# Summing the two parts of VectorE's exponentials with accumulating DMAs in a two-layer transformer kernel

## The chip, the cores and the metric

The kernel runs on one core of a Trainium2 chip. Five engines work beside each other, each with an instruction queue of its own that it follows in order: TensorE (PE: matmuls, and PEld: the loading of their weights), ScalarE (ACT), VectorE (DVE), GpSimd (POOL) and SyncE (SP, which only issues DMAs). Sixteen DMA engines move the data. Engines wait for each other by semaphores. The metric is the device time of one execution in microseconds (us).

## What is computed

Two transformer layers, one after the other, with the same weights, over 2048 rows of 448 numbers in bf16. Each layer is an attention block and a dense block, each behind a layer norm:

```python
qkv = (x @ wqkv).reshape(B, S, 3, H, Dh)          # B=1, S=2048, H=16, Dh=28
scores = jnp.einsum("bhqd,bhkd->bhqk", q, k) * scale
p = _softmax(scores, axis=-1)
o = jnp.einsum("bhqk,bhkd->bhqd", p, v)           # then @ wo
...
h = jnp.einsum("bsd,df->bsf", x, w1) + b1         # F=1792
r = jnp.where(h > zero, h, zero)
out = jnp.einsum("bsf,fd->bsd", r * r, w2) + b2
...
x = x + _A_ref(_layernorm(x), A_wqkv, A_wo)
x = x + _B_ref(_layernorm(x), B_w1, B_b1, B_w2, B_b2)
```

and the last two lines once more. The exponentials of the softmax are the largest single piece: 2 layers x 16 heads x 2048 x 2048 of them.

## The kernel before

**Tiling.** The 16 heads are four groups of four; each head has 32 rows of the 128 partitions. The queries are cut in blocks of 256 rows (the last ones of layer two in 128). A *pass* is one query block of one head group over some of the keys. A *unit* or *part* is one head's 512 columns of scores: 128 keys on the partitions, two key blocks of 256 queries beside each other. There are 2048 parts.

**A group.** `s_stream` puts two or three parts into a group. TensorE writes their scores into one PSUM tile `sc` of three banks (line 1154; two such tiles exist), and ScalarE turns the tile into exponentials `pt` in SBUF with one instruction (line 1192: 1024 columns for two parts, 1536 for three). TensorE may compute the same scores twice (`again`, limited by MORE), which keeps it at work. The value matmuls (line 1380) multiply the exponentials with the values and sum over the keys in PSUM, four heads beside each other.

**VectorE's parts.** In some groups the third part does not go to ScalarE. `apart` decides it: by lists of group numbers (FORCE, SKIP), by VectorE's load and by the memory cells that are free. For such a part VectorE builds the exponential from the bits of the number. Line 1216 (or 1214) reads the scores and writes a 16-bit integer `z`. From there the exponential is made as a **sum of two bf16 tiles**: `x2`, a product, and `z`, in which only the exponent bits are left. There are two ways to them. In `a_rest` GpSimd (at times VectorE) computes a bent copy (line 1263), a fraction (line 1269) and the new `z` (line 1274), and VectorE multiplies (line 1278). In `a_whole` VectorE does all of it: lines 1232, 1236 and 1239. Which one it is depends on PLIM, a limit on the work queued for GpSimd. Each of `z` and `x2` lies in a cell of 512 columns: in buffers of their own (`v_c`), in parts of K, Q and V tiles that are not needed at the time, or, for `z`, in the unused third of `pt`.

**The two reads.** Nothing adds the two tiles. TensorE multiplies both with the same values and lets PSUM add: `z` with the other parts at line 1380, and `x2` in batches of its own at line 1345, when at least XMIN heads have one ready. The variables `known`, `more` and `batch` in `p_stream` keep the account of the second read.

**The order of the work.** A planner in the kernel's file simulates all engines with a price for each operation and writes out one fixed order for each engine. Every operation is an `Op` with an engine, a duration, what it depends on, and the cells it holds (`acq`, `rel`). `lat` is a time between its end and the moment when others may use it. Streams of operations have priorities; of those that can go on, the one that could start first is taken. A set of constants steers the choice (how full VectorE may be, how long parts wait, how many cells are kept), and `PACE` changes them from group to group. An operation with `port=True` takes turns between VectorE and GpSimd. On the chip only the order and the semaphores are left, not the planned times.

**DMAs.** SyncE issues the loads, the stores of the output, and for each pair of head groups three small steps for the softmax's denominator (lines 1480, 1491, 1499). GpSimd issues none. Besides its part of the exponentials GpSimd computes the root of the layer norms (line 673).

**Stages.** An opening until the first exponential; then attention of both layers with the dense blocks mixed in; and a tail in which the last rows go through the dense block. The last 80 parts (STOP) all go to ScalarE.

Of the kernel before, what the change touches and what calls it, by code (L numbers as in the profile page):

```python
# [13 lines left out]
ALU = mybir.AluOpType  # L14
# [16 lines left out]
PLIM = 99.0  # L31
OVER = 0.0825
EDUR = 0.617
# [5 lines left out]
XMIN = 4  # L39
HELD = 0.14  # L40
# [105 lines left out]
FORCE = (22, 27, 31, 36, 64, 104, 108, 120, 122, 156, 162, 192, 196, 233, 235, 237, 254, 263, 287, 292, 301, 306,  # L146
         329, 341, 392, 408, 430, 445, 466, 501, 515, 553, 556, 567, 577, 593, 598, 602)
SKIP = (20, 29, 46, 135, 184, 195, 216, 222, 242, 262, 280, 282, 320, 321, 378, 388, 395, 404, 406, 409, 416, 418,
        433, 440, 446, 479, 500, 512, 526, 544, 574, 601, 609, 621, 622, 646, 652, 663)
PACE = {  # L150
    0: {'BUSY': 0.95, 'LOW': 0.7, 'CHUNK': 1, 'EV': 2.9, 'FAR': 6, 'KEEP': 5, 'LAG': 8, 'LEAD': 18, 'MARGIN': 3,
         'MORE': 3, 'PRE': 0.5, 'SLACK': 0.7, 'SPAN': 8, 'TB': 2.4, 'TB2': 2.4, 'V_AGE': 5, 'V_LAST': 3, 'V_PAST':
         2, 'C_PRIO': 1.6, 'V_PRIO': 4, 'V_LATE': 2.6, 'V_WAIT': 5, 'ASIDE': 1, 'XMIN': 4, 'HOLD': 6, 'LADD': 0.05,
         'RES': 2, 'RES2': 2, 'TASIDE': -0.2, 'EPRIO': 2.6, 'SPARE': 0, 'NEAR': 3, 'SOON': 1, 'VGAP': 0.03, 'PWAIT':
         0.3, 'PNEAR': 0.2, 'PORTP': 1, 'PLIM': 99.0},
    8: {'LEAD': 12, 'BUSY': 0.9, 'PLIM': 2},
    16: {'SPAN': 11},
    24: {'LAG': 3},
    32: {'PLIM': 2.6, 'EV': 3.5},
    40: {'TB2': 3.0},  # L160
    42: {'BUSY': 0.95, 'CHUNK': 3, 'EV': 2.9, 'LAG': 8, 'LEAD': 18, 'MORE': 1, 'SPAN': 8, 'TB': 1.6, 'TB2': 2.4,
         'V_PRIO': 8.5},
    56: {'BUSY': 1.0, 'LAG': 3},
    64: {'NEAR': 9, 'ASIDE': 0.2, 'LADD': 0.1},
    72: {'V_AGE': 4},
    88: {'V_AGE': 3},
    112: {'C_PRIO': 1.2, 'HOLD': 5},
    120: {'LEAD': 10, 'LAG': 12, 'SPARE': 3, 'ASIDE': 2},
    128: {'TB': 2.0, 'MORE': 3},
    136: {'PRE': 1.2, 'MARGIN': 6},  # L170
    144: {'EPRIO': 4},
    152: {'CHUNK': 1, 'VGAP': 0},
    160: {'BUSY': 0.95, 'V_PRIO': 4, 'V_PAST': 3},
    168: {'RES': 1, 'C_PRIO': 2.1, 'LOW': 1.0},
    176: {'EV': 2.2, 'TB2': 2.0, 'LOW': 0.5},
    192: {'PORTP': 0.3, 'SOON': 0.6},
    200: {'CHUNK': 2, 'PRE': 0.3},
    208: {'PNEAR': 0.25, 'V_AGE': 6},
    216: {'NEAR': 3},
    248: {'EPRIO': 6},  # L180
    256: {'ASIDE': 0},
    264: {'MARGIN': 10},
    280: {'PORTP': 2},
    288: {'HOLD': 6},
    296: {'TB': 1.0, 'PNEAR': 0.15},
    304: {'SPAN': 6},
    312: {'BUSY': 1.0},
    320: {'LEAD': 12, 'MARGIN': 6},
    328: {'V_LATE': 6},
    336: {'LOW': 1.0},  # L190
    360: {'PNEAR': 0.05, 'TB': 2.4, 'V_LATE': 2.6, 'V_AGE': 3},
    368: {'C_PRIO': 1.6},
    376: {'PNEAR': 0.15, 'V_PRIO': 8.5},
    384: {'XMIN': 3, 'LEAD': 18},
    392: {'CHUNK': 3},
    400: {'KEEP': 6, 'ASIDE': 4, 'V_AGE': 6, 'BUSY': 0.9},
    408: {'PWAIT': 0.6, 'MORE': 1},
    424: {'RES': 2, 'BUSY': 1.0},
    440: {'HEAT': 0.6, 'WINDOW': 3.4, 'CHUNK': 2},
    456: {'V_AGE': 5, 'TB': 1.3},  # L200
    480: {'TB': 1.6, 'PORTP': 0.3, 'PLIM': 2},
    488: {'LADD': 0.2, 'HOLD': 4},
    496: {'MARGIN': 3, 'PNEAR': 0.35},
    504: {'PWAIT': 0.3},
    512: {'KEEP': 4, 'EV': 2.9},
    520: {'V_AGE': 4, 'C_PRIO': 1.2, 'HOLD': 5},
    528: {'PRE': 0.8},
    536: {'XMIN': 4, 'SPAN': 15, 'ASIDE': 2, 'PRE': 0.3},
    544: {'V_AGE': 5, 'EV': 2.2},
    552: {'PORTP': 1, 'LEAD': 12, 'FAR': 17, 'PRE': 0},  # L210
    560: {'V_LATE': 6, 'VGAP': 0.03},
    568: {'SPARE': 0, 'NEAR': 9},
    576: {'SOON': 1.5, 'PNEAR': 0.15},
    584: {'PLIM': 1.3, 'LAG': 3, 'V_WAIT': 3},
    592: {'KEEP': 6, 'V_LAST': 2.2},
    600: {'V_AGE': 8},
    608: {'EV': 1.3, 'LOW': 0.8},
    616: {'PRE': 1.2, 'BUSY': 0.95, 'V_PAST': 2, 'FAR': 6},
    624: {'LADD': 0.1, 'BUSY': 0.9},
    648: {'PRE': 0.5, 'SPAN': 20, 'EV': 3.5, 'ASIDE': 0.2},  # L220
    656: {'ASIDE': 1, 'SLACK': 0.4},
    672: {'SOON': 1, 'ASIDE': 0.2},
    680: {'SLACK': 0.7},
# [183 lines left out]
def kernel(  # L407
# [819 lines left out]
    def a_whole(gi, c, unit):  # L1227
# [14 lines left out]
        o = Op("DVE", 0.42, close, deps=[h], sets=("x", gi), port=True)  # L1242
        w = Op("DVE", TDUR, whole, deps=[o], sets=("w", gi), port=True)
# [6 lines left out]
        left[0] -= 0.34  # L1250

    def a_rest(gi, c, unit):
# [39 lines left out]

    norm_done = {}
    rows_done = set()
# [400 lines left out]
```

## Time and profile before

| | before |
|---|---|
| time, median of 2 runs | 803.53 us (803.46 to 803.6) |
| time of the profiled execution | 803.48 us |
| its span, first to last instruction | 801.7 us |
| TensorE's granted clock | 1.00 |
| instructions | 29246 |
| DMA traffic | 18.13 MB, 23 GB/s over the span |
| exponentials on ScalarE (line 1192) | 683, 776.6 us |
| parts on VectorE (lines 1214, 1216) | 337 |

A share of the span tells how full an engine is, not whether it sets the end. For that the idle time of each engine has to be placed: where it lies, and what ended it. Groups of instructions come with their busy time, the mean length of one in ns and the engine's idle time just before them. Neighbouring instructions of one engine may overlap in the records; a busy time of a group counts covered time once, a mean does not. Instructions that only issue a DMA or wait for a semaphore are not counted as busy. "issue" is time in which an engine waited for nothing that the profile shows.

### The profile page before, as it was taken

The page shows a single profiled execution, that of the slowest core. Times are in us where ns is not written, and L with a number is a line of the kernel's source. Part 1 is how long each engine was busy: PE and PEld are TensorE (multiplying, and loading weights), DVE is VectorE, ACT ScalarE, POOL GpSimd, SP SyncE. Part 2 cuts the span into 40 slices and gives each one's busy share as a digit, 9 for nine tenths or more (in the row PEclk, how much of TensorE's full clock was granted, in tenths as well). Part 3 has the DMA queues.
Part 4 walks back from the last instruction along what each step waited for, and adds up shares of the span by engine and source line. Part 5 has one row for each costly group of instructions (what it writes and reads, how often), then busy time and mean ns, then how long its engine had stood idle before and what let it go on. Part 6 is the DMA issues. An engine that isn't in the chain of part 4 may idle for free.

```text
span 801.7 us, 29246 instructions
## 1 busy us (share of the span) xinstructions
PE 778.7 (97%) x12242; PEld 417.6 (52%) x12242; DVE 744.8 (93%) x1818; ACT 789.4 (98%) x702; POOL 454.7 (57%) x717
## 2 busy tenths in 40 slices
PE   9999989999999999999999999989999999999998
PEld 6555545544555545555455545445454544545666
DVE  8999999999999999999999998999999999989564
ACT  8999999999999999999999999999999999999995
POOL 3346777657676664544566657657665566654200
PEclk9999999999999999999999999999999999999999
DMA  9300010000000000000000000011100000000100
GB/s 250 86 2 2 5 34 23 17 16 16 17 3 16 16 16 16 3 16 15 2 3 2 3 2 2 15 32 30 33 11 22 21 28 21 22 23 9 27 8 19
DMA packets 32480, 18.13 MB, mean 23 GB/s; under 512 B 17818, under 2 KB 31899, under 8 KB 32348
## 3 DMA queue, kind: packets, MB, share of 16 engines
q1 hardware_dynamic: 32204, 16.16, 7.4%
q8 instruction: 95, 1.56, 0.8%
q14 instruction: 37, 0.30, 0.1%
q10 hardware_dynamic: 144, 0.11, 0.0%
HBM read 13.98 MB, written 2.06 MB: 20 GB/s over the span
## 4 chain that ended last, share of the span: by engine, by line
PE 41%; ACT 33%; DVE 17%; issue 8%; DMA 0%; POOL 0%; ACTq 0%; DVEq 0%
ACT pt L1192 33%; PE mt L809 19%; PE sc L1154 12%; PE oT L1380 7%; DVE pt L1216 2%; DVE r L1584 2%; PE oT L1345 1%; DVE pt L1214 1%; DVE V_sb L1591 1%; DVE K_sb L1278 1%; DVE v_c L1278 1%; DVE v_c L1216 1%; PE tp L712 1%; DVE x_sb L1513 1%; PE sc L809 1%
## 5 line engine op out<-in xcount | busy, mean ns | idle before, releaser
L1192 ACT ACTIVATE pt<-sc 128x1536 bf16<-128x1536 f32 (+1 forms) x683 | 776.6, 1292 | 1.2 <-PE sc L1154 0.9
L1154 PE MATMUL sc<-Q_sb,K_sb 32*128 32x256 bf16 (+1 forms) x4652 | 279.6, 265 | 15.7 <-ACT pt L1192 13.5
L1154 PEld LDWEIGHTS <-K_sb 32*128 32x128 bf16 x4652 | 101.1, 92 | 186.3 <-issue 118.3
L1380 PE MATMUL oT<-pt,V_sb 128*32 128x256 bf16 (+1 forms) x4000 | 167.8, 268 | 0.5 <-DVE Q_sb L828 0.3
L1380 PEld LDWEIGHTS <-V_sb 128*32 128x32 bf16 x4352 | 101.5, 96 | 45.3 <-issue 35.9
L809 PE MATMUL mt<-xnT,w 128*128 128x256 bf16 (+1 forms) x904 | 119.6, 270 | 0.9 <-DVE xnT L724 0.2
L1274 POOL TENSOR_SCALAR pt<-pt 128x512 int16<-128x512 int8 x131 | 83.9, 642 | 39.9 <-ACT pt L1192 5.7
L809 PEld LDWEIGHTS <-w 128*128 128x128 bf16 x952 | 78.0, 98 | 35.2 <-issue 26.4
L1216 DVE TENSOR_SCALAR pt<-sc 128x512 int16<-128x512 f32 x132 | 89.8, 684 | 2.3 <-PE sc L1154 1.6
L1584 DVE TENSOR_SCALAR r<-mt 128x512 bf16<-128x512 f32 (+1 forms) x107 | 73.0, 682 | 3.8 <-PE mt L809 3.4
L673 POOL TENSOR_TENSOR rstd<-mv,mhalf 128x2 f32<-128x2 f32 (+1 forms) x34 | 25.4, 747 | 76.4 <-DVE mv L676 48.2
L809 PE MATMUL mt<-w,V_sb 128*128 128x448 bf16 (+2 forms) x288 | 66.5, 345 | 0.0
L1274 POOL TENSOR_SCALAR v_c<-v_c 128x512 int16<-128x512 int8 x64 | 42.8, 668 | 24.5 <-DVE V_sb L1269 4.3
L1269 POOL TENSOR_SCALAR v_c<-pt 128x512 f16<-128x512 uint8 x57 | 37.8, 663 | 31.9 <-DVE K_sb L1263 5.8
L1513 DVE TENSOR_TENSOR x_sb<-x_sb,mt 128x448 bf16<-128x448 bf16 x61 | 37.4, 612 | 12.9 <-PE mt L809 12.6
L1216 DVE TENSOR_SCALAR v_c<-sc 128x512 int16<-128x512 f32 x69 | 46.6, 682 | 0.7 <-PE sc L1154 0.6
L648 DVE BATCH_NORM_STATS2 st<-x_sb 128x6 f32<-128x448 bf16 x63 | 38.9, 619 | 0.7 <-DMA x_sb<-in_A_x_dram 0.5
L809 PEld LDWEIGHTS <-V_sb 128*128 128x128 bf16 x302 | 25.4, 98 | 24.4 <-issue 10.0
L1345 PE MATMUL oT<-v_c,V_sb 128*32 128x256 bf16 (+1 forms) x298 | 35.0, 273 | 0.0
L1591 DVE TENSOR_TENSOR V_sb<-r 128x512 bf16<-128x512 bf16 x70 | 29.2, 421 | 3.0 <-ACT r L1582 2.8
L1274 POOL TENSOR_SCALAR K_sb<-K_sb 128x512 int16<-128x512 int8 x39 | 25.3, 650 | 11.2 <-DVE v_c L1278 2.4
L1269 POOL TENSOR_SCALAR K_sb<-pt 128x512 f16<-128x512 uint8 x35 | 23.9, 682 | 13.2 <-DVE pt L1216 4.3
(219 smaller groups left out, 1254.0 us busy)
## 6 DMA issues: line engine op xcount, KB each, us to landing
rec<-scr SPq DMA_DIRECT2D x54, 128.0 KB
out_dram<-x_sb SPq DMA_DIRECT2D x15, 112.0 KB
x_sb<-in_A_x_dram SPq DMA_DIRECT2D x7, 224.0 KB
w<-in_B_w_dram SPq DMA_DIRECT2D x1, 1568.0 KB
w<-in_B_w_dram SPq DMA_DIRECT2D x1, 1344.0 KB
dn<-oT_sb SPq DMA_DIRECT2D x54, 4.0 KB
V_sb<-in_A_wqkv_dram SPq DMA_DIRECT2D x4, 168.0 KB
scr<-dn SPq DMA_DIRECT2D x27, 8.0 KB
```

Source lines behind the costliest of these rows:

```text
L648: nc.vector.bn_stats(out=box["st"][:, :], in_=x_sb[:, t0 + j, :] if src is None else src())
L809: nc.tensor.matmul(box["t"][:, c0:c0 + n], lhsT=lhsT() if callable(lhsT) else lhsT, rhs=rhs, start=a, stop=b)
L1154: nc.tensor.matmul(dst[k][:, i * nt * P:(i + 1) * nt * P], lhsT=K_sb[l][rows, g, (kb + i) * P:(kb + i + 1) * P], rhs=Q_sb[rows, g, t0 * P: ...
L1192: t = nc.scalar.activation(out=pt[:, 0:n], in_=gbuf[gi]["sc"][:, 0:n], func=AF.Exp, scale=float(np.log(2.0)) * 2.0 ** -FRAC)
L1216: t = nc.vector.tensor_scalar(out=z.bitcast(DT.int16), in0=src, scalar1=2.0, scalar2=EXP_BIAS, op0=ALU.mult, op1=ALU.add)
L1269: on(e).tensor_scalar(out=box["f"], in0=gbuf[gi]["z"].bitcast(DT.uint8).rearrange("p (n t) -> p n t", t=2)[:, :, 0], scalar1=2.0 ** -9, sc ...
L1274: on(e).tensor_scalar(out=gbuf[gi]["z"].bitcast(DT.int16), in0=gbuf[gi]["z"].bitcast(DT.int8).rearrange("p (n t) -> p n t", t=2)[:, :, 1], ...
L1345: nc.tensor.matmul(box["t"][DHP * hh:DHP * hh + DHP, 0:n], lhsT=V_sb[l][:, kb + i, 4 * g + hh, :], rhs=gbuf[gi]["x2"][:, i * n:(i + 1) * n ...
L1380: nc.tensor.matmul(box["t"][DHP * hh:DHP * hh + DHP, 0:n], lhsT=V_sb[l][:, tb, 4 * g + hh, :], rhs=p, start=begin and j < G, stop=close an ...
L1513: nc.vector.tensor_tensor(out=x_sb[:, tb, lo:hi], in0=x_sb[:, tb, lo:hi] if src is None else src[:, lo:hi], in1=t[:, 0:hi - lo], op=ALU.add)
L1584: nc.vector.tensor_scalar(out=r[:, 0:w], in0=t[:, 0:w], scalar1=0.0, scalar2=None, op0=ALU.max)
L1591: nc.vector.tensor_tensor(out=h[:, 0:w // n, :], in0=r, in1=r, op=ALU.mult)
```

## The change

The two tiles of a VectorE part are added in memory, and the value matmuls read the sum once. A new function `summed` waits for the last of VectorE's operations of the part (`o` and `w`) and lets GpSimd issue a DMA that reads `x2` and adds it to `z` in SBUF. The planner prices this with ADUR = 0.62 us on GpSimd, `port=True`, and a token `("w", gi)` that comes ALAT = 2.0 us later; the value matmul at line 1380 waits for that token. The cell of `x2` becomes free with it. The token `("x", gi)` no longer exists, and with `not ACC` in `p_stream` no second read is ever put down, so the batches of line 1345 are gone.

The constants that steer the planner are chosen anew: FORCE goes from 38 to 22 groups, SKIP from 37 to 21, and PACE has fewer and other entries. PLIM is 1.2 from group 24 on, -1 from 408 to 527 (every part goes through `a_whole` there), and 1.2 again after that; before it was 2 or 2.6 from group 8 on and 1.3 from group 584 on.

```diff
+ACC = 1
+ADUR = 0.62
+ALAT = 2.0
...
-        o = Op("DVE", 0.42, close, deps=[h], sets=("x", gi), port=True)
-        w = Op("DVE", TDUR, whole, deps=[o], sets=("w", gi), port=True)
+        o = Op("DVE", 0.42, close, deps=[h], sets=() if ACC else ("x", gi), port=True)
+        w = Op("DVE", TDUR, whole, deps=[o], sets=() if ACC else ("w", gi), port=True)
...
+        if ACC:
+            pl.spawn(EPRIO, summed(gi, h, o, w))
+
+    def summed(gi, t, o, w):
+
+        def acc(e):
+            nc.gpsimd.dma_start(out=gbuf[gi]["z"], in_=gbuf[gi]["x2"], accum_op=ALU.add)
+        a = Op("POOL", ADUR, acc, deps=[o, w], port=True)
+        yield a
+        d = Op("-", 0.0, None, deps=[a], rel=t, lat=ALAT, sets=("w", gi))
+        d.dur = 0.0
+        yield d
...
-        w = Op(("POOL", "DVE"), (EDUR, 0.42), whole, deps=[t, h], sets=("w", gi), port=True)
-        o = Op("DVE", 0.42, close, deps=[t, h], rel=h, sets=("x", gi), port=True)
+        w = Op(("POOL", "DVE"), (EDUR, 0.42), whole, deps=[t, h], sets=() if ACC else ("w", gi), port=True)
+        o = Op("DVE", 0.42, close, deps=[t, h], rel=h, sets=() if ACC else ("x", gi), port=True)
...
+        if ACC:
+            pl.spawn(EPRIO, summed(gi, t, o, w))
...
-                        if k == 3 and gi not in known:
+                        if k == 3 and gi not in known and not ACC:
```

What the two built programs hold, by count:

| | before | after |
|---|---|---|
| exponentials on ScalarE, 1536 columns | 345 | 370 |
| exponentials on ScalarE, 1024 columns | 338 | 313 |
| parts on VectorE | 337 | 312 |
| of these wholly on VectorE (`a_whole`) | 67 | 194 |
| GpSimd's 128x512 operations (bent, fraction, whole) | 141, 249, 264 | 69, 118, 118 |
| accumulating DMAs issued by GpSimd | 0 | 312 |
| value matmuls | 5034 | 4352 |
| score matmuls (4096 without repeats) | 4652 | 4994 |

More of the change, by code (lines that the diff above doesn't have):

```diff
@@ L145 @@
 QP = 6
[L146 to L149, printed above, removed]
+FORCE = (56, 61, 87, 129, 131, 154, 238, 360, 397, 412, 436, 441, 453, 524, 528, 573, 575, 588, 603, 604, 623, 630)
@@ L153 @@
          2, 'C_PRIO': 1.6, 'V_PRIO': 4, 'V_LATE': 2.6, 'V_WAIT': 5, 'ASIDE': 1, 'XMIN': 4, 'HOLD': 6, 'LADD': 0.05,
[L154 removed]
+         'RES': 2, 'RES2': 2, 'TASIDE': -0.2, 'EPRIO': 2.6, 'SPARE': 0, 'NEAR': 3, 'SOON': 1, 'VGAP': 0, 'PWAIT':
          0.3, 'PNEAR': 0.2, 'PORTP': 1, 'PLIM': 99.0},
[L156 to L159, printed above, removed]
@@ L215 @@
[L215 to L223, printed above, removed]
+    8: {'NEAR': 9, 'HOLD': 3, 'LADD': 0.2},
+    16: {'TB': 2.0},
+    24: {'PLIM': 1.2},
+    42: {'MORE': 1, 'TB': 1.6, 'V_PRIO': 8.5, 'NEAR': 3, 'VGAP': 0.03, 'HOLD': 6, 'LADD': 0.05},
@@ new lines @@
+    48: {'CHUNK': 1},
+    80: {'SLACK': 0.4, 'MORE': 3},
+    88: {'SLACK': 0.5},
+    104: {'V_LAST': 2.5},
+    120: {'MARGIN': 6},
+    128: {'NEAR': 6},
+    136: {'MORE': 1},
+    144: {'KEEP': 6, 'PNEAR': 0.15},
+    152: {'LAG': 20},
+    160: {'LOW': 1.0},
+    168: {'LEAD': 15},
+    176: {'V_LATE': 4.6},
+    192: {'RES2': 4, 'SOON': 0.6, 'C_PRIO': 2.1},
+    200: {'V_WAIT': 7, 'SLACK': 0.7},
+    216: {'SPAN': 20},
+    256: {'BUSY': 1.0, 'C_PRIO': 1.2},
+    264: {'EV': 1.3},
+    272: {'VGAP': 0},
@@ new lines @@
+    280: {'LOW': 0.8},
+    288: {'SLACK': 0.5},
+    296: {'KEEP': 4, 'SPARE': 3},
+    304: {'BUSY': 0.9},
+    312: {'SPAN': 6, 'LEAD': 10, 'NEAR': 9},
+    328: {'C_PRIO': 1.6, 'LADD': 0.1},
+    352: {'BUSY': 1.06},
+    360: {'V_LAST': 3.5},
+    408: {'PLIM': -1, 'PRE': 0.8},
+    424: {'SOON': 1.5},
+    432: {'TB2': 2.0},
+    448: {'PRE': 0},
+    464: {'TB2': 0.6},
+    472: {'V_LAST': 3, 'C_PRIO': 1.2},
+    480: {'TB2': 1.4},
+    488: {'PRE': 1.2},
+    512: {'RES2': 6},
+    528: {'SPAN': 8, 'PLIM': 1.2},
@@ L224 @@
+    536: {'RES': 1, 'FAR': 12, 'LEAD': 15},
+    544: {'VGAP': 0.06},
+    592: {'PNEAR': 0.35},
+    600: {'LAG': 24},
+    608: {'BUSY': 0.95},
+    616: {'V_LAST': 3.5},
+    624: {'LADD': 0.2},
 }
```

60 lines of the change are left out of this document (3 added, 57 removed).

## The prediction

> **What bounds the kernel now.** I read the busy shares first, then ScalarE's steps in order of time, then the chain of waits, then the lines of the work that the change touches. Durations are those of the one profiled execution: its span is 801.7 us and its own time 803.48 us, so 1.8 us lie around the span, and it stands 0.05 us under the median of the runs shown, 803.53 us.
>
> The busy shares of the page:
>
> ```profile
> span 801.7 us, 29246 instructions
> ...
> PE 778.7 (97%) x12242; PEld 417.6 (52%) x12242; DVE 744.8 (93%) x1818; ACT 789.4 (98%) x702; POOL 454.7 (57%) x717
> ```
>
> Three engines look full. The order of time of ScalarE tells which of them sets the end (columns: start, length, then what ran; the idle time ahead in brackets):
>
> ```profile
> 9.28 7.07 ACT L1192 ACTIVATE pt<-sc 128x1536 bf16<-128x1536 f32 x5
> ...
> 749.79 37.29 ACT L1192 ACTIVATE pt<-sc 128x1536 bf16<-128x1536 f32 x28
> 788.24 0.60 ACT L1582 ACTIVATE r<-sc 128x512 bf16<-128x512 f32 x1 [1.15 <-PE sc L809]
> ```
>
> The exponentials of line 1192 begin at 9.28 us and end at 749.79 + 37.29 = 787.08 us. The rest is an opening of 9.3 us and a tail of 801.7 - 787.1 = 14.6 us. The groups by shape (last numbers: busy time, mean ns, idle time before):
>
> ```profile
> L1192 ACT ACTIVATE pt<-sc 128x1536 bf16<-128x1536 f32 x345 | 490.1, 1504 | 0.6 <-PE sc L1154 0.5
> L1192 ACT ACTIVATE pt<-sc 128x1024 bf16<-128x1024 f32 x338 | 338.4, 1076 | 0.6 <-PE sc L1154 0.4
> ```
>
> Between 9.28 and 787.08 us ScalarE is idle for 0.6 + 0.6 = 1.2 us. Neighbours overlap, so the two busy times do not add; together they cover 777.8 - 1.2 = 776.6 us. This stretch is ScalarE's. The difference of the means, 1504 - 1076 = 428 ns, is what one more part of 512 columns costs it. How much waiting hides inside the steps? In the run of 28 above, 27 are wide and the last is narrow in the built order. Without the first one's 1.50 us, 35.79 us are 26 wide steps and a narrow one, so 27 wide steps are 36.2 us: 1.341 us a wide step, 0.913 us a narrow one. At this pace all exponentials would take 345 x 1.341 + 338 x 0.913 = 771.2 us. So 776.6 - 771.2 = 5.4 us of waiting are hidden, and 6.6 us with the idle time is all that better feeding could give back.
>
> The chain that ended last, by engine, seems to say otherwise:
>
> ```profile
> PE 41%; ACT 33%; DVE 17%; issue 8%; DMA 0%; POOL 0%; ACTq 0%; DVEq 0%
> ```
>
> It walks through TensorE for 41% of the span because TensorE's order is written out and each of its instructions follows another; it says who was the last to hand over, not who has no room. I come back to it as a rival.
>
> **What the change moves.** I count instructions in the two built programs. An attention part is one head's 128x512 block; there are 2048 of them. Before, 345 x 3 + 338 x 2 = 1711 go to ScalarE and 337 to VectorE. After, it is 370 wide and 313 narrow exponentials, 1736 parts, and 312 for VectorE. The number of steps stays 683. So the kernel that relieves TensorE gives VectorE less, not more: **ScalarE gets 25 x 0.428 = 10.7 us.** Nothing hides it, as ScalarE has no idle time in its stretch. That is the main term.
>
> **VectorE and GpSimd.** The totals by line (columns: stretch, its length, busy time with count for VectorE, and for GpSimd where a second pair stands, then clock, DMA share and GB/s), in the order L1216, L1214, L1232, L1236, L1239, L1263, L1269, L1274, L1278:
>
> ```profile
> 0.00:801.70 801.70, 183.45 (x270) 1.00 0.08 23
> 0.00:801.70 801.70, 45.43 (x67) 1.00 0.08 23
> 0.00:801.70 801.70, 19.33 (x67) 1.00 0.08 23
> 0.00:801.70 801.70, 29.50 (x67) 1.00 0.08 23
> 0.00:801.70 801.70, 21.17 (x67) 1.00 0.08 23
> 0.00:801.70 801.70, 37.00 (x129) 94.88 (x141) 1.00 0.08 23
> 0.00:801.70 801.70, 8.84 (x21) 162.69 (x249) 1.00 0.08 23
> 0.00:801.70 801.70, 2.50 (x6) 170.54 (x264) 1.00 0.08 23
> 0.00:801.70 801.70, 113.19 (x270) 1.00 0.08 23
> ```
>
> VectorE before: 183.5 + 45.4 + 19.3 + 29.5 + 21.2 + 37.0 + 8.8 + 2.5 + 113.2 = 460.4 us. After, 194 parts go wholly through VectorE (lines 1232, 1236, 1239: 0.29 + 0.44 + 0.32 = 1.05 us) where 67 did, and 118 go with GpSimd: 312 x 0.679 = 211.9, 194 x 1.05 = 203.7, 49 x 0.287 = 14.1 and 118 x 0.419 = 49.4, together 479.1 us. That is 19 us more in a longer span, 763.5 of 812.4, 94%. It costs nothing as long as ScalarE is the slower one; without that cover it would be these 19 us.
>
> GpSimd loses 141 + 249 + 264 - (69 + 118 + 118) = 349 operations: 428.1 us become 69 x 0.673 + 118 x 0.653 + 118 x 0.646 = 199.7 us. It gains 312 issues of accumulating DMAs, which no row shows. The nearest rows are SyncE's issues below, 0.36 to 0.55 us, and GpSimd's own 128x512 operations, 0.65 us. I take 0.65: 203 us, so GpSimd stays where it was, at 226.3 + 203 = 429 of 812 us. It would be full only from (812.4 - 226.3) / 312 = 1.88 us an issue. Behind a waiting issue stand the other GpSimd parts and the 34 roots of the layer norms; GpSimd's 43% idle time covers them.
>
> **TensorE.** The second read of a VectorE part (line 1345) goes, 682 matmuls; line 1154, the scores, grows from 4652 to 4994, because it repeats scores where TensorE would be idle. Totals of line 1345, then of line 1154 (TensorE, then weight loads):
>
> ```profile
> 0.00:801.70 801.70, 49.81 (x682) 23.02 (x682) 1.00 0.08 23
> ```
>
> ```profile
> 0.00:801.70 801.70, 279.58 (x4652) 101.07 (x4652) 1.00 0.08 23
> ```
>
> That is -49.8 + 342 x 0.060 = -29.3 us. TensorE's idle time goes from 23.0 us to about 812.4 - 749.4 = 63 us. Off the path it is worth nothing by itself; it can only thin out the 6.6 us that ScalarE loses to feeding. I take a third of that: **-2.2 us** (bounds 0 and -6.6).
>
> **The new wait.** The one remaining read of a VectorE part now waits for a DMA. The order of TensorE is built on 0.62 us for the issue and 2.0 us to the landing, and a value matmul may be put down the moment this 2.62 us is over. What the landing really takes, no row shows. The nearest (SyncE's issues; VectorE's use of the loaded tile):
>
> ```profile
> 212.64 0.36 SPq L1491 DMA_DIRECT2D scr<-dn  x1
> 214.99 1.11 SPq L1499 DMA_DIRECT2D rec<-scr  x2
> ```
>
> ```profile
> 220.73 0.68 DVE L1504 TENSOR_TENSOR oTn<-oT_sb,rec 128x512 bf16<-128x512 f32 x1
> ```
>
> An 8 KB store is waited for until 2.35 us after its issue; two loads of 128 KB are used 5.7 us after the first issue, 5.2 after the second. Of the size I learn from the opening:
>
> ```profile
> 0.00:10.00 10.00, 8.19 (x91) 7.10 (x91) 6.75 (x31) 8.53 (x11) 4.45 (x11) 1.00 0.76 207
> ```
>
> 207 GB/s at a share of 0.76 would be 272 GB/s, so 128 KB take 0.48 us, twice that if both operands pass. My estimate is 2.35 + 0.7 = 3.05 us, between 2.35 and 5.2, nearer the store because one transfer is small: 0.43 us later than the order expects. The Trainium skill, page "DMA: Bandwidth & Descriptors", section "Anatomy of one DMA — SWDGE (gpsimd) path", fits a DMA from GpSimd with 2.0 us plus bytes over 436 GB/s; by that the landing is at 2.3 us, the sums are on time and the total is 812. No run here shows it yet.
>
> How many reads does it hit? When parts are in time, value reads hardly wait for data:
>
> ```profile
> L1380 PEld LDWEIGHTS <-V_sb 128*32 128x32 bf16 x4352 | 101.5, 96 | 45.3 <-issue 35.9 <-DVE oT_sb L1405 0.7 <-DVE v_c L1278 0.6
> ...
> L1345 PEld LDWEIGHTS <-V_sb 128*32 128x32 bf16 x682 | 23.0, 96 | 11.1 <-issue 10.5
> ```
>
> All but 9.4 + 0.6 = 10.0 us of their idle time is issue. In the built order the value matmul of a VectorE part now stands 15 groups of scores behind its own scores (median; 7 at least) instead of 10 (4 at least). At 776.6 / 683 = 1.14 us a group that is 17 us, against some 0.7 + 1.05 + 0.65 + 3.05 = 5.4 us of work on a part, so most reads have room. I choose that one in eight is at the tight end: 39 x 0.43 = 17 us of TensorE standing still. Behind a waiting value matmul stand the next scores, and behind them ScalarE's next exponential, which is then late. Before, 23.0 us of idle TensorE went with at most 6.6 us lost by ScalarE, 0.29 of it. So **+5 us**; bounds 0 (all on time) and 312 x 0.43 x 0.29 = 39 us (all hit).
>
> DMA engines: 312 x 131 KB x 2 at 272 GB/s are 300 us of traffic, 37% of the span beside 8% now; the normalisers' loads share it and have 5 us of use behind them. I put it at nothing. No part of VectorE falls into the tail, before or after: the last 80 parts are barred from it by the code.
>
> **Sum.** 803.5 + 10.7 - 2.2 + 5 = **817 us**, 1.7% over before.
>
> **Rivals.** *On time.* The sums land within 2.62 us: 803.5 + 10.7 - 2.2 = 812; between 803.5 + 10.7 - 6.6 = 807.6 and 815. For it: the comfortable distance of 15 groups.
>
> *GpSimd's issues are held up by VectorE, and the kernel is clearly slower.* The place is the issue itself. The row that bears on it, duration as least, median and greatest ns:
>
> ```profile
> L1274 POOL TENSOR_SCALAR pt<-pt x131: 612/618/1498, 47.6 to 748.8; 128x512 int16<-128x512 int8 x131
> ```
>
> A GpSimd operation can be stretched from 612 to 1498 ns beside VectorE, though the median hardly moves. If an issue is stretched as far, 1.5 us, GpSimd has 226 + 468 = 694 us of 812, queues form, and sums are 0.88 + 0.43 = 1.3 us late. With a quarter of the reads hit it is 78 x 1.3 x 0.29 = 29 us: 803.5 + 10.7 + 29 = 843. It decides from about 0.25 us of lateness beyond mine (39 x 0.25 x 0.29 = 2.8 us), where the total passes 2%. Against it: the median of 618. The Trainium skill, page "SBUF — State Buffer", section "SBUF: two separate sides", speaks against this change: GpSimd cannot write descriptors while VectorE holds the shared port, and a DMA of 620 ns alone took 3100 ns. By that alone 312 issues would be 967 us, more than the span; the 1498 ns above agree in kind, the median does not.
>
> *TensorE was the bound.* If the chain's 41% meant that, the kernel would fall by 29.3 us to 774. ScalarE's floor forbids it: 9.3 + 370 x 1.341 + 313 x 0.913 + 14.6 = 805.9 us of span, 807.7 us of time. It needs shorter exponentials than any run of steps here shows.
>
> **Chances.** Sums a little late, as forecast: 0.43, with its own range 812 to 824, of which 0.17 lies above 819.6. On time: 0.27. Issues held up: 0.25. TensorE the bound: 0.02. A tail or opening some us shorter, 803 to 808: 0.03. A difference of 2% (787.5 to 819.6 us) is about what I treat as told from no change: faster 0.02; the same 0.27 + 0.26 + 0.03 = 0.56; slower 0.17 + 0.25 = 0.42. The range from 808 to 836 leaves out about 0.05 below and half of the held-up case above.
>
> **What would show it.** 683 exponentials whose covered time is about 787 us and an idle time of a few us say that the main term is right; exponentials that wait for TensorE, and value loads that wait for a DMA, say that the sums are late, with the size of the new wait. GpSimd's issue rows give its price: near 0.6 us, or above 1. It would be wrong if the exponentials began much later than 9.3 us or the tail were not near 14.6 us, if ScalarE's idle time went beyond 10 us, or if the landing took less than 2.6 us.

## The result, and the profile after

| | before | after |
|---|---|---|
| time, median of 2 runs | 803.53 us | 861.04 us (860.94 to 861.13) |
| span of the profiled execution | 801.7 us | 859.2 us |
| ratio of the times | | 1.0716, 95% interval 1.067 to 1.0762 |

The changed kernel is slower by 57.5 us. The prediction said 817 us and a range up to 836: the time lies above all of it.

The head of the changed kernel's page: busy time of each engine, the granted clock in 40 slices, and the two queues that carry the traffic (packets, MB, share of 16 engines).

```profile
span 859.2 us, 28809 instructions
...
PE 788.3 (92%) x11896; PEld 412.7 (48%) x11896; DVE 768.5 (89%) x1914; ACT 806.4 (94%) x703; POOL 511.7 (60%) x680
...
PEclk9999979999999999999999999989999999999999
...
q0 software_dynamic: 44928, 40.91, 31.3%
q1 hardware_dynamic: 32204, 16.16, 7.1%
...
DVE 28%; PE 25%; ACT 20%; DMA 14%; issue 9%; POOL 4%; SPq 0%; POOLq 0%; ACTq 0%; DVEq 0%
...
L1172 ACT ACTIVATE pt<-sc 128x1536 bf16<-128x1536 f32 (+1 forms) x683 | 793.5, 1315 | 41.6 <-PE sc L1134 39.8
```

The last line is the one to read first. ScalarE's 683 exponentials are busy for 793.5 us, which is not far from the 787 that the prediction named. But the idle time in front of them is 41.6 us, where it was 1.2, and 39.8 of it ends with scores that TensorE delivers late. In the chain (second line from below) DMA stands with 14%; before, no DMA had a share worth naming. The opening and the tail did not move, as ScalarE's first and last stretches show (timeline of the changed kernel; start, length, operation, count):

```profile
9.31 7.08 ACT L1172 ACTIVATE pt<-sc 128x1536 bf16<-128x1536 f32 x5 [0.20 <-PE sc L1134]
...
806.91 37.29 ACT L1172 ACTIVATE pt<-sc 128x1536 bf16<-128x1536 f32 x28 [0.47 <-PE sc L1134]
```

The exponentials begin at 9.3 us, and the last ends at 844.2, 15.0 us ahead of the end. So all of the loss lies between. From the end of one exponential to the end of the next, ScalarE's usual step is still 1.343 us for 1536 columns and 0.917 for 1024. Summed over the trace, its steps exceed that pace by 50.8 us, idle time and hidden waiting together; before, it was 4.4.

What holds TensorE up is told by the view of line 1237, the issue of the accumulating DMAs (durations as least, median and greatest ns; two of its 19 groups of tiles):

```profile
L1237 POOL DMA_DIRECT2D v_c<-v_c x55: 854/883/1221, 38.2 to 795.0; - x55
...
L1237 POOL DMA_DIRECT2D K_sb<-v_c x30: 854/1041/1487, 227.3 to 797.7; - x30
...
who waited for it (us, times):
  PE oT L1374: 30.8, 31
  PEld L1374: 4.1, 3
...
DMA to landing us min/median/max: 2.6/2.9/6.6
```

Three of these 34 waits stand at the weight load, and two of the three stand a second time at the matmul behind it. Counted once, TensorE stood still for 32 of the sums, 31.6 us in all. Over the 312 issues the least is 0.852 us and the mean 0.956. From the start of an issue to the landing it takes 2.58 us at least, 2.85 at the median, 4.50 at the 90th percentile and 6.6 at most. The order was built on 2.62.

The dearest of these waits shows how it spreads (timeline of the changed kernel, the lines around it):

```profile
385.61 1.11 SPq L1493 DMA_DIRECT2D rec<-scr  x2
...
386.19 0.86 POOL L1237 DMA_DIRECT2D pt<-v_c  x1 [1.04 <-DVE xn L752]
...
391.98 0.40 PE L1374 MATMUL oT<-pt,V_sb 128*32 128x256 bf16 x7 [3.29 <-DMA pt<-v_c]
...
392.81 1.02 ACT L1172 ACTIVATE pt<-sc 128x1024 bf16<-128x1024 f32 x1 [3.18 <-PE sc L1134]
392.82 0.69 DVE L1196 TENSOR_SCALAR pt<-sc 128x512 int16<-128x512 f32 x1 [2.97 <-PE sc L1134]
```

SyncE issues two loads for a normaliser at 385.6 us, GpSimd its sum half a microsecond later. The matmul that reads the sum starts 5.8 us after the issue and has waited 3.29 us. The next scores stand behind it in TensorE's queue. ScalarE then has waited 3.18 us and VectorE 2.97: nearly one to one. Of the 312 sums, the 73 issued from 2 us before to 3.5 us after the issue of such a load take 4.16 us at the median, the others 2.72. Nine of the 73 are waited for, and they make up 17.1 of the 31.6 us.

### The profile page after: what moved, and what is told of

Read it like the earlier page. It is cut to its first block, busy times and chain, and to the rows that moved or that the text cites. A ratio compares the mean times of both kernels' runs of the same rounds, so it can differ in the third digit from the quotient of the medians.

```text
span 859.2 us, 28809 instructions
## 1 busy us (share of the span) xinstructions
PE 788.3 (92%) x11896; PEld 412.7 (48%) x11896; DVE 768.5 (89%) x1914; ACT 806.4 (94%) x703; POOL 511.7 (60%) x680
## 3 DMA queue, kind: packets, MB, share of 16 engines
q0 software_dynamic: 44928, 40.91, 31.3%
## 4 chain that ended last, share of the span: by engine, by line
DVE 28%; PE 25%; ACT 20%; DMA 14%; issue 9%; POOL 4%; SPq 0%; POOLq 0%; ACTq 0%; DVEq 0%
ACT pt L1172 20%; PE mt L789 9%; PE sc L1134 7%; PE oT L1374 7%; DMA pt<-v_c 3%; DVE r L1578 2%; DVE v_c L1194 2%; DMA pt<-V_sb 2%; DVE x_sb L1507 2%; DVE st L628 1%; DMA v_c<-v_c 1%; DMA rec<-scr 1%; DVE K_sb L1194 1%; DMA K_sb<-v_c 1%; DVE v_c L1216 1%
## 5 line engine op out<-in xcount | busy, mean ns | idle before, releaser
L1172 ACT ACTIVATE pt<-sc 128x1536 bf16<-128x1536 f32 (+1 forms) x683 | 793.5, 1315 | 41.6 <-PE sc L1134 39.8
L1134 PEld LDWEIGHTS <-K_sb 32*128 32x128 bf16 x4994 | 117.8, 93 | 208.3 <-issue 132.3
L1237 POOL DMA_DIRECT2D v_c<-v_c x55 | 50.4, 922 | 46.2 <-DVE v_c L1219 14.8
L1578 DVE TENSOR_SCALAR r<-mt 128x512 bf16<-128x512 f32 x106 | 72.1, 681 | 4.5 <-PE mt L789 4.1
L789 PE MATMUL mt<-w,V_sb 128*128 128x448 bf16 (+1 forms) x288 | 70.9, 350 | 0.0
L1194 DVE TENSOR_SCALAR v_c<-sc 128x512 int16<-128x512 f32 x71 | 48.4, 682 | 3.6 <-PE sc L1134 3.2
L1194 DVE TENSOR_SCALAR K_sb<-sc 128x512 int16<-128x512 f32 x60 | 41.0, 683 | 3.8 <-PE sc L1134 3.6
L1237 POOL DMA_DIRECT2D K_sb<-K_sb x33 | 31.5, 955 | 19.1 <-DVE h L1212 3.2
L1237 POOL DMA_DIRECT2D v_c<-K_sb x30 | 27.6, 932 | 22.5 <-DVE v_c L1212 5.4
L1237 POOL DMA_DIRECT2D K_sb<-v_c x30 | 31.9, 1065 | 10.1 <-issue 2.6
L789 PEld LDWEIGHTS <-V_sb 128*128 128x128 bf16 x302 | 24.6, 97 | 24.6 <-issue 12.2
L1196 DVE TENSOR_SCALAR v_c<-sc 128x512 int16<-128x512 f32 x46 | 31.3, 681 | 3.0 <-PE sc L1134 3.0
```

What stands on the lines that cost most here:

```text
L789: nc.tensor.matmul(box["t"][:, c0:c0 + n], lhsT=lhsT() if callable(lhsT) else lhsT, rhs=rhs, start=a, stop=b)
L1134: nc.tensor.matmul(dst[k][:, i * nt * P:(i + 1) * nt * P], lhsT=K_sb[l][rows, g, (kb + i) * P:(kb + i + 1) * P], rhs=Q_sb[rows, g, t0 * P: ...
L1172: t = nc.scalar.activation(out=pt[:, 0:n], in_=gbuf[gi]["sc"][:, 0:n], func=AF.Exp, scale=float(np.log(2.0)) * 2.0 ** -FRAC)
L1194: t = nc.vector.tensor_scalar(out=z.bitcast(DT.int16), in0=src, scalar1=EXP_WHOLE, scalar2=0.0, op0=ALU.add, op1=ALU.max)
L1196: t = nc.vector.tensor_scalar(out=z.bitcast(DT.int16), in0=src, scalar1=2.0, scalar2=EXP_BIAS, op0=ALU.mult, op1=ALU.add)
L1237: nc.gpsimd.dma_start(out=gbuf[gi]["z"], in_=gbuf[gi]["x2"], accum_op=ALU.add)
```

## The experiments

All line numbers are those of the changed kernel. Each experiment was run once. The kernel before, run beside it on the same chip, took 803.42 to 803.69 us.

**The theory** after this reading: the reads of the sums come too early for the landings, and this is most of the 57.5 us. **The rivals:** the new pace is bad by itself; the issues cost more on GpSimd than planned; the traffic disturbs other transfers.

**1. Sums that nothing reads.**

```diff
-            nc.gpsimd.dma_start(out=gbuf[gi]["z"], in_=gbuf[gi]["x2"], accum_op=ALU.add)
+            nc.gpsimd.dma_start(out=gbuf[gi]["x2"], in_=gbuf[gi]["z"], accum_op=ALU.add)
```

> The accumulating DMA runs as in the changed kernel, issued at the same place by GpSimd and with the same bytes, but it adds z to x2 instead of x2 to z. Nobody reads x2 afterwards, so the value matmul reads z and waits only for the engine that wrote it. The second part of each exponential is left out of the result. All five orders are the same as in the changed kernel. Landing theory (the 57 us are the value matmuls' wait for sums that land late, passed on to ScalarE): ScalarE's idle time falls from 41.6 us to under 10 and the time to 815 to 826 us. GpSimd theory (its issues of 0.96 us and its slowed operations delay the parts themselves, whoever waits for the sum): the issues still cost the same, so it stays above 845 us. Pace theory (the new order is bad in itself): it stays at 855 to 861 us.

Measured: 831.34 us, 29.7 below the changed kernel. The group of the exponentials in this run:

```profile
L1172 ACT ACTIVATE pt<-sc 128x1536 bf16<-128x1536 f32 (+1 forms) x683 | 790.2, 1362 | 15.1 <-PE sc L1134 10.7
```

Waiting for landings is worth 29.7 us: half of the loss, not nearly all of it, and the time lies between those that the theories gave. Some 28 us over the kernel before remain with no read waiting for a sum. (ScalarE still waits twice, 2.2 us together, for DMAs that have yet to read a `pt` tile.)

**2. The new pace without the sums.**

```diff
-ACC = 1
+ACC = 0
```

> The new constants of the planner with the accumulating DMAs switched off: both tiles are read by value matmuls as before the change. VectorE gets 321 parts here (337 in the kernel before, 312 in the changed one), so ScalarE has 361 wide and 322 narrow exponentials, some 6.8 us more than before. Pace theory: above 840 us, as the order is bad without the DMAs too. Landing theory and GpSimd theory: 807 to 815 us, the kernel before and the 6.8 us.

Measured: 876.00 us. This tells nothing of the pace as it is used: the planner's prices change with ACC, 321 parts go to VectorE, and one hole makes up most of the time, two of ScalarE's waits (timeline of this run):

```profile
446.37 1.94 ACT L1172 ACTIVATE pt<-sc 128x1024 bf16<-128x1024 f32 x2 [32.59 <-PE sc L1134]
...
462.27 38.03 ACT L1172 ACTIVATE pt<-sc 128x1024 bf16<-128x1024 f32 x33 [13.96 <-PE sc L1134]
```

The constants belong to one set of prices. The expectation was missed, and the run leaves the question open.

**3. Thin loads for the normaliser.** Each of the loads behind which sums arrive late brings 32 columns (DHP) in place of 256, and the multiplication takes the first of them for all.

```diff
-                nc.sync.dma_start(out=box["r"][:, i, 0:n], in_=src.unsqueeze(1).to_broadcast([G, DHP, n]))
+                nc.sync.dma_start(out=box["r"][:, i, 0:DHP], in_=src[:, 0:DHP].unsqueeze(1).to_broadcast([G, DHP, DHP]))
...
-                                                                   in1=box["r"][:, :, 0:n], op=ALU.mult)
+                                                                   in1=box["r"][:, 0:1, 0:1].to_broadcast([P, 2, n]), op=ALU.mult)
```

> The changed kernel, but the two loads that spread a softmax denominator over the partitions fetch 32 columns instead of 256 (an eighth of the bytes), and the multiplication takes one column for all; the normalisation is left out of the result. All orders and the accumulating DMAs stay the same. Landing theory in the form that the late landings are collisions with these loads on the DMA engines (the landings of 4.5 to 6.6 us stand beside them): the 90th percentile of the landing falls from 4.5 to about 3.3 us, the waits of 2 to 3 us go, and the time falls by 15 to 25 us to 836 to 846 us. If the collisions do not matter (GpSimd theory or pace theory): 857 to 861 us.

Measured: 845.11 us, 15.9 below the changed kernel. The waits for the sums in the view of line 1237:

```profile
who waited for it (us, times):
  PE oT L1374: 20.2, 33
  PEld L1374: 0.9, 3
...
DMA to landing us min/median/max: 2.6/2.8/4.9
```

There are as many waits, but they are shorter: counted once, 35 sums and 20.9 us instead of 32 and 31.6. The 90th percentile of the landings falls from 4.50 to 3.78 us, and only 9 of them take over 4.5 us instead of 32. So the normaliser's loads make most of the longest landings. How much of the 15.9 us comes from that, run 8 tells. **Control:** the same edit in the kernel before.

> The control for the thin loads: the kernel before with the normaliser's loads cut to an eighth and one column taken for all (the normalisation is left out of the result). If the loads cost the kernel time by themselves, it falls below 800 us and the 15.9 us of the same step in the changed kernel are not all the sums' doing. If they are in time there, as VectorE never sits idle for them: 803 to 804 us.

Measured: 803.56 us. Without sums beside them these loads cost nothing.

**4. A longer landing in the planner's prices.**

```diff
-ADUR = 0.62
-ALAT = 2.0
+ADUR = 0.95
+ALAT = 3.5
```

> The changed kernel with truer prices in the planner: 0.95 us for the issue and 3.5 us to the landing (4.45 together, in place of 2.62). The value matmuls are put down later, and VectorE gets 318 parts, so ScalarE's work is 2.6 us less than in the changed kernel. Landing theory: nearly all landings of the changed kernel lie below 4.5 us, so most waits go: 815 to 832 us. GpSimd theory: the issue has its price now but GpSimd's own operations are still slower than planned: about 840 us. Pace theory: 850 us and more.

Measured: 897.28 us. The waits for landings fell to 7.0 us in 6 reads, as they should. Two others took their place (list of waits: us, times, longest):

```profile
ACT pt L1172 <- PE sc L1134: 40.3, 21, 7.0
...
ACT pt L1172 <- PE oT L1374: 35.3, 26, 3.5
```

The second line is of a new kind: ScalarE waits for value matmuls that still hold its `pt` tiles. I take it that a read put off holds all the tiles of its batch for longer. The expectation was missed; with these constants a better price gives a worse order. What an order searched with the new prices would win is not shown.

**5. No sum at all.** This run splits what remains.

```diff
-            nc.gpsimd.dma_start(out=gbuf[gi]["z"], in_=gbuf[gi]["x2"], accum_op=ALU.add)
+            pass
```

> The changed kernel's orders on all engines with the accumulating DMAs left out altogether: GpSimd issues nothing, nothing is added, the value matmul reads z alone (the second part is left out of the result). What is left over the kernel before is the 10.7 us of ScalarE's additional parts, the longer way of 194 parts on VectorE, and the order itself. Of the 57.5 us, 29.7 went when only the wait for the sum was taken away, so 17.1 us beside the 10.7 are open. If GpSimd's issues cause them (its queue and the port): 814 to 820 us. If the order itself, or VectorE's additional work, causes them: 827 to 832 us.

Measured: 812.84 us. The engines and the exponentials in this run:

```profile
PE 768.7 (95%) x11896; PEld 411.8 (51%) x11896; DVE 746.0 (92%) x1914; ACT 798.2 (98%) x703; POOL 235.7 (29%) x368
...
L1172 ACT ACTIVATE pt<-sc 128x1536 bf16<-128x1536 f32 (+1 forms) x683 | 785.2, 1415 | 1.6 <-PE sc L1134 1.4
```

The order itself has no fault: ScalarE idles for 1.6 us. It is 9.4 us slower than before because ScalarE has 25 more parts. The rival of the bad pace falls.

**6. Sums of 16 columns, not read.**

```diff
+            nc.gpsimd.dma_start(out=gbuf[gi]["x2"][:, 0:16], in_=gbuf[gi]["z"][:, 0:16], accum_op=ALU.add)
```

> As the run in which the sum is unread (z added to x2, nobody waits; the second part is left out of the result), but each DMA moves 16 of the 512 columns: GpSimd issues 312 DMAs, while the traffic on the DMA engines is a thirty-second. If the issue costs what it costs by the number of rows and not of bytes, it stays near 0.9 us. If GpSimd's queue is what is left of the 17 us: 828 to 832 us, as with whole tiles. If the traffic is (the normalisers' loads come late behind the sums): below 822 us.

Measured: 822.86 us, 10.0 over no sum and between the two expectations. Its engines and exponentials:

```profile
PE 771.0 (94%) x11896; PEld 411.2 (50%) x11896; DVE 766.5 (93%) x1914; ACT 801.3 (98%) x703; POOL 512.6 (62%) x680
...
L1172 ACT ACTIVATE pt<-sc 128x1536 bf16<-128x1536 f32 (+1 forms) x683 | 788.3, 1374 | 7.6 <-PE sc L1134 6.1
```

An issue is as long as with 512 columns: 0.852 us at least, 0.963 in the mean. So its length comes from the issue and not from the bytes. Beside the issues VectorE is busy for 20.5 us more, and GpSimd's own operations of lines 1255, 1261 and 1266 take 249.2 us instead of 204.6, though the instructions are the same; this comes back below.

**7. The pace of before with the sums.** FORCE, SKIP and PACE are those of the kernel before, ACC stays 1.

> The accumulating DMAs with the constants of the kernel before: the change without its new pace. VectorE gets 358 parts (337 before, 312 in the changed kernel), so ScalarE has 324 wide and 359 narrow exponentials, 9 us less than before and 19.7 us less than in the changed kernel. If the landings set the loss alone, whatever the pace: about 861 - 20 = 841 us. If the order must be searched for the prices it is built on: above 861 us, with single holes of many us. Only if neither matters: 795 us.

Measured: 1032.52 us, with 358 parts on VectorE. Line 1374 waits 50.1 us for landings; the rest of the 230 us is other holes in the order. Like run 2, it shows that constants searched for one set of prices say nothing under another.

**8. Runs 1 and 3 together**, sums of whole tiles that nothing reads, beside thin loads.

> Sum unread and the normaliser's loads cut to an eighth, both at once (the second part and the normalisation are left out of the result). The two steps took 29.7 and 15.9 us alone. If the thin loads help only by bringing the sums' landings forward, nothing is left for them to gain here: 829 to 832 us. If the sums hold up the normalisers' loads too, which then come late for VectorE: 818 to 826 us.

Measured: 820.57 us, 10.8 below run 1. Here no read waits for a sum, so most of this is what the sums do to the normaliser's loads (ScalarE's waits for a DMA that reads a `pt` tile fall from 2.2 to 0.5 us besides). In run 1 the list of waits has a row for it, in which VectorE waits with the multiplication by the loaded tile (us, times, longest):

```profile
DVE oTn L1498 <- DMA rec<-scr: 5.6, 7, 2.3
```

In the kernel before, line 1504, the same operation, waits for nothing.

Runs 1, 3 and 8 together say what run 3 alone does not. Reading the sums costs 845.11 - 820.57 = 24.5 us beside thin loads and 29.7 beside whole ones. So 10.8 of the 15.9 us of run 3 come without any read of a sum, only some 5 come with the reads, and most of the price of reading stays when the collision with these loads is gone.

**9. Sums of 16 columns, read and waited for.**

```diff
+            nc.gpsimd.dma_start(out=gbuf[gi]["z"][:, 0:16], in_=gbuf[gi]["x2"][:, 0:16], accum_op=ALU.add)
```

> As the changed kernel, the value matmul waiting for the landing, but each DMA adds 16 of the 512 columns (the rest of the second part is left out of the result). Against the run of tiny sums that nobody reads (822.9 us) only the wait is added; against the changed kernel only the traffic is gone. There the tiny landings took 2.03 us from the start of the issue at the median, 3.7 at the 90th percentile; the order is built on 2.62. If the 29.7 us of waiting come from the length of the landings and their collisions: 823 to 830 us. If they come from parts that reach GpSimd's queue late, whatever the landing: 840 us and more.

Measured: 841.76 us, 18.9 over run 6. By the expectation, a time above 840 us speaks for parts that reach GpSimd's queue late; the waits below do not bear that out. (The 2.03 us called a median there is the lower quartile; the median of run 6 is 2.27.) The waits in this run:

```profile
who waited for it (us, times):
  PE oT L1374: 14.0, 16
  PEld L1374: 10.2, 9
...
DMA to landing us min/median/max: 2.0/2.2/4.9
```

Eight of these waits stand twice; counted once, 17 sums are waited for, 17.5 us. The usual landing, 2.2 us, is well inside the 2.62 of the order. The tail does it: the 90th percentile is 3.8 us, and 14 of the 17 sums, with 15.3 of the 17.5 us, take over 3.1 us to land. So the length of the landings counts, but it hardly comes from the bytes. Shrinking the bytes by 32 takes away only 10.8 of the 29.7 us that reading costs.

**10. GpSimd adds the two tiles itself**, with no DMA.

```diff
+            nc.gpsimd.tensor_tensor(out=gbuf[gi]["z"], in0=gbuf[gi]["z"], in1=gbuf[gi]["x2"], op=ALU.add)
```

> The changed kernel's orders, but GpSimd adds the two tiles itself (one tensor_tensor of 128x512 in place of the DMA); the result is the reference's. GpSimd's two-operand operation on 128x448 took 1.13 us in the kernel before, so I expect 1.1 to 1.3 us for it, more than an issue's 0.96, but the sum is ready at its end instead of 3.2 us after its start (mean), and nothing is moved by the DMA engines. If landing and traffic are most of the loss (29.7 + 8.5 of 48 us): 822 to 832 us. If GpSimd's occupied time is: 850 us and more, as it would rise by some 50 us.

Measured: 902.76 us, on the side of "850 us and more". The add takes 1.157 us at the median, 376 us in all. But GpSimd is busy for only 67% of the span; it is VectorE that becomes the limit:

```profile
PE 782.6 (87%) x11896; PEld 405.3 (45%) x11896; DVE 855.0 (95%) x1914; ACT 819.2 (91%) x703; POOL 607.4 (67%) x680
...
DVE 74%; PE 10%; ACT 6%; issue 5%; POOL 3%; DMA 1%; SPq 0%; ACTq 0%; DVEq 0%; POOLq 0%
```

VectorE has the same 1914 instructions for 855.0 us instead of 746.0. As a test of the landings the run fails, since it brings a dearer trouble of its own. It shows where that comes from; the totals of two of VectorE's lines, first line 1216 (product, operands and result in SBUF), then line 1194 (reads PSUM), 194 operations each, in run 5, the changed kernel and run 10:

```profile
0.00:1000.00 1000.00, 79.32 (x194) 1.00 0.07 18
```

```profile
0.00:1000.00 1000.00, 84.31 (x194) 0.98 0.34 59
```

```profile
0.00:1000.00 1000.00, 109.91 (x194) 0.99 0.07 18
```

```profile
0.00:1000.00 1000.00, 132.15 (x194) 1.00 0.07 18
```

```profile
0.00:1000.00 1000.00, 132.08 (x194) 0.98 0.34 59
```

```profile
0.00:1000.00 1000.00, 130.87 (x194) 0.99 0.07 18
```

The product grows from 79.3 / 194 = 0.41 us to 0.43 beside the issues and 0.57 beside GpSimd's adds. The read of PSUM stays at 0.68.

**11. Is it the clock?** In the changed kernel TensorE's granted clock falls to 0.50 in eight stretches, 34.1 us together (the expectation below says 40, which is too much); seven begin within 1.7 us of the end of a wait of 1.1 to 3.3 us for a landing. One of them in two views of the changed kernel, the timeline of TensorE and the windows around it (in the windows: length, busy time of PE, PEld, DVE, ACT and POOL, granted clock, DMA share, GB/s):

```profile
649.87 0.40 PE L1134 MATMUL sc<-Q_sb,K_sb 32*128 32x256 bf16 x6
653.16 1.90 PE L1374 MATMUL oT<-pt,V_sb 128*32 128x256 bf16 x32 [2.90 <-DMA pt<-h]
654.99 0.61 PE L1134 MATMUL sc<-Q_sb,K_sb 32*128 32x256 bf16 x6
```

```profile
650.00:653.00 3.00, 0.26 (x6) 0.09 (x1) 2.37 (x10) 2.08 (x2) 0.54 (x2) 1.00 0.47 90
653.00:657.00 4.00, 3.84 (x58) 2.11 (x57) 0.37 (x1) 1.30 (x1) 1.20 (x2) 0.57 0.45 69
657.00:661.00 4.00, 4.00 (x39) 1.45 (x38) 3.90 (x11) 3.60 (x5) 0.00 (x0) 1.00 0.00 0
```

Six score matmuls take 0.61 us instead of 0.40, and ScalarE is busy for 1.30 of 4 us. The Trainium skill, page "TensorE: Matmul & The Clock Gate", section "What's actually happening", says that the array's clock is halved after an idle window of some 3.4 us and back after a busy one. The trace agrees on the half and on the length (seven of the eight stretches cost 1.7 us of full clock, which is 3.4 us at half, the eighth three times as much), but full idleness is not needed: TensorE was busy for 0.6 to 2.0 of the 3.4 us ahead of the eight. The steps of ScalarE that touch these stretches exceed its pace by 23.3 of the 50.8 us. To tell price from company, zeros are multiplied where TensorE had waited:

```diff
+                        for f in range(FILL.get(count[0], 0)):
+                            new = begin and j < G
+                            q = todo[j + f % (G - j)][1] if new else f % G
+                            nc.tensor.matmul(box["t"][DHP * q:DHP * q + DHP, 0:n], lhsT=none[:], rhs=wv[:, 0, 0:n],
+                                             start=new, stop=new, tile_position=(0, DHP * q))
```

> The changed kernel; at the 24 value matmuls which stood still for 0.45 us or more in its profiled run (29.0 us together), TensorE now multiplies zeros for nearly as long before it waits: 498 matmuls of 128x256 at about 0.05 us each, 25 us, which add nothing to the sums. The landings stay as late as they were. What changes is that TensorE is not idle while they are awaited. In the changed kernel the granted clock falls to 0.50 for 3.4 us or more in eight stretches, 40 us together, seven of them right behind a wait of 1.1 to 3.3 us for a landing, and ScalarE loses 22.4 of its 50.8 us in them. Theory that half of the price of a late landing is the clock it costs: the clock stays at 1.00 in most of the run, and of these 22.4 us about 10 to 20 come back: 841 to 852 us. Rival, the slow stretches only go along with the waits, and the lateness alone is the price: the clock may stay up, but the time is 857 to 866 us, since what TensorE multiplies takes as long as the wait did. If the added matmuls push scores back, it is above 866 us.

Measured: 862.84 us. The mean granted clock rises from 0.980 to 0.992, two slow stretches of 13.7 us together are left instead of eight of 34.1, and the time does not fall. This is the rival's time: it speaks for the lateness itself as the price. The run is not quite clean. Landings shifted: they were still waited for, 24.6 us, at other places too, and 12 of the 24 places had no wait left behind the added work. It took 8.3 us there, part of which may have come on top. If all of it did, the stretches that went were worth 8.3 - 1.8 = 6.5 us, not the 10 to 20 expected.

## Why the prediction was wrong, point by point

The runs stand in a row, each with one thing more than the one before it. Run 9 gives the other way round: with 16 columns the waiting costs 18.9 us, and whole tiles then 19.3 more. So the shares of traffic and waiting depend on the order of the steps; the sum does not.

| | time | step | |
|---|---|---|---|
| before | 803.4 | | |
| new order, no sums (run 5) | 812.8 | +9.4 | ScalarE's 25 more parts |
| with 312 sums of 16 columns, unread (run 6) | 822.9 | +10.0 | the issues, with 4 KB each |
| whole tiles, unread (run 1) | 831.3 | +8.5 | the traffic |
| whole tiles, read: the change | 861.0 | +29.7 | waits for landings |

**The main term** was right. 10.7 us for ScalarE's parts, with 2.2 us back, is 8.5; run 5 has 9.4, and its steps exceed ScalarE's pace by 2.8 us instead of 4.4, so 1.6 of the 2.2 us came back there. The opening and the tail are where they were put. The time that the rival "on time" gave, 812, is that of run 5: it would have come true had the sums cost nothing at all.

**TensorE's relief** was rightly put off the path, but it was smaller than reckoned: its busy time fell by 10.0 us in run 5, not by 29.3. (The rows of its lines overlap: before, those of lines 1154, 1345, 1380 and 809 add up to 864.6 us where it is busy for 778.7, so differences of rows overstate.) In the changed kernel its idle time is 859.2 - 788.3 = 70.9 us instead of 23; much of that is waiting for the sums.

**The new wait, the step that failed most:** "39 x 0.43 = 17 us of TensorE standing still", passed on at 0.29, so 5 us. It cost 29.7 us. Three factors made the term, and the runs have 32, 0.99 us and 0.94 for them:
- How many reads are hit: one in eight, 39, was chosen without a row to rest on; 32 waited. Near, by luck.
- How late: 3.05 us to the landing was the estimate, 0.43 late. The median of 2.85 is even sooner. But the reads that wait are mostly those whose landing is in the tail: they wait 31.6 / 32 = 0.99 us each, and 18 of the 32, with 24.2 us, belong to landings over 3.1 us. I took one value where a distribution decides. (The other 14, with 7.3 us, landed in the usual time. Late issues are the likely cause; no run shows it.) Over half of the waiting stands beside the normaliser's loads, and the prediction had both transfers in its hands without asking what the loads do to the sums. They are not the only source: with thin loads 20.9 us of waiting are left, and reading still costs 24.5 us. What delays the rest stays open. The Trainium skill's fit in "DMA: Bandwidth & Descriptors", section "Anatomy of one DMA — SWDGE (gpsimd) path", gave 2.3 us; the least is 2.58 here, and 1.96 for 16 columns, so it is near a floor and says nothing of the tail.
- What ScalarE gets of it: 0.29 came from all of TensorE's idle time before. But 13.5 of those 23.0 us ended with ScalarE: TensorE was ahead there, and its idle time cost nothing. The line of the kernel before that says so:

```profile
L1154 PE MATMUL sc<-Q_sb,K_sb 32*128 32x256 bf16 (+1 forms) x4652 | 279.6, 265 | 15.7 <-ACT pt L1192 13.5 <-DVE st L648 0.3
```

  A wait for a landing is passed on nearly whole: 29.7 / 31.6 is 0.94, and the stop of 3.29 us ahead of the scores was 3.18 us for ScalarE. I put this down to the two `sc` tiles, the only buffer between TensorE and ScalarE; no run has more of them.

**GpSimd's issues** were put at 0.65 us and at nothing, covered by its idle time. They take 0.956 us, 298 us in all, and their presence costs 10.0 us although GpSimd is at 60%. Being idle 40% of the time did not cover them. Two things are seen in run 6 against run 5: GpSimd's own operations, 44.6 us longer and behind the issues in its queue, and VectorE's 20.5 us of longer operations. The prediction had 19 us more for VectorE too, but for another reason, the longer way of 194 parts; run 5, which has that way, shows only 746.0 - 744.8 = 1.2. How the 10.0 us divide between them no run shows.

**The traffic** was put at nothing. Its share came out near (37% estimated, 31.3% measured), but by luck: the page counts 40.91 MB, half of the bytes reckoned, at 152 GB/s instead of 272. Its cover was wrong: the "5 us of use behind" the normaliser's loads did not hold. Whole tiles cost 8.5 us unread, and run 8 gives back 10.8 by making these loads thin. In run 1 part of it comes with two slow stretches of the clock (its slices show 8 and 7), of which run 8 has none; how much of the 8.5 us that is, no run shows.

**The rival "issues held up"**, 843 with 0.25, was on the right side for a wrong reason. It needed VectorE to stretch an issue from 0.65 to 1.5 us. An issue takes 0.85 at least and 0.88 at the median, 1.58 at most in one case, and the long delays come between the issue and the landing. The Trainium skill ("SBUF — State Buffer", section "SBUF: two separate sides") gives its 3100 ns for a whole DMA and not for the issue, as the prediction took it; no issue here comes near it, and the median landing of 2.85 us stays below it. What the prediction lacked is a rival in which several transfers meet.

**No version that beats both** came out of this. Run 5, with the sums left out, is 9.4 us slower than before already, because the 312 parts leave ScalarE 25 more. As long as the order has that number, sums at no price would lose.

## What to carry to other kernels

An asynchronous step that a queue in strict order waits for is priced by the tail of its landing and not by the median; look for the other transfers in flight at that moment, and ask how deep the buffers are between the waiting engine and the one that sets the end: here, with two, 31.6 us of stops cost 29.7. Test such a collision with and without the wait, since taking it away can help by another way too (10.8 of the 15.9 us here). An engine that is idle 40% of the time need not hide 300 us of issues: its own and its neighbour's operations grew beside them. And count first what the change takes from the engine that sets the end: here the best case was already a loss.

## What the runs showed of the hardware

- Issuing an accumulating DMA keeps GpSimd for 0.852 us at least, for 16 columns as for 512.
- Its landing goes by company more than by bytes: 2.27 us at the median for 4 KB and 2.85 for 128 KB, but 4.16 for 128 KB when a load of SyncE's queue is issued near it, and up to 6.6.
- VectorE's product from SBUF to SBUF becomes longer beside GpSimd, by 6% beside issues and by 39% beside adds of two operands (line 1216: 79.3, 84.3, 109.9 us); its reads of PSUM do not (line 1194: 132.2, 132.1, 130.9 us).
- GpSimd's own operations become longer beside its issues, 249.2 us instead of 204.6 for the same 305 operations (run 6 against run 5), and not beside its adds (206.7 us in run 10).
- TensorE's clock was halved, for 3.4 us or a multiple, behind 3.4 us in which TensorE was still busy for 0.6 to 2.0 us.
